# Attention ahead of two mixtures: two key blocks packed into one by an elementwise maximum, a third PSUM bank for products with v, gates and rank, and the rank behind the next scores

## The chip, the cores and the metric

One core of a Trainium2 chip runs the whole program. The metric is device time in microseconds (us), the median of several executions. The trace is one profiled execution of the kernel before; its times count from the first instruction. TensorE is called PE here, VectorE DVE, ScalarE ACT, GpSimd POOL, and SP is the engine that issues most DMAs.

## What is computed

Attention over 4 sequences of 576 positions with 8 heads of 64, causal within a window of 128 positions and with a slope per head, then a mixture with one chosen expert per row, then a mixture over four experts. The change touches the attention alone.

```python
def _attn_ref(q, k, v):
    B, H, S, D = q.shape          # 4, 8, 576, 64
    scores = (1.0 / np.sqrt(D)) * np.matmul(q, k.transpose(0, 1, 3, 2))
    rel = pos[:, None] - pos[None, :]
    bias = slopes[:, None, None] * (-np.abs(rel))[None, :, :]
    mask = (rel >= 0) & (rel < 128)
    scores = np.where(mask, scores + bias[None], -1000000000.0)
    attn = np.exp(scores - np.max(scores, axis=-1, keepdims=True))
    attn = attn / (np.sum(attn, axis=-1, keepdims=True) + 1e-09)
    return np.matmul(attn, v)
```

With a window of 128 and tiles of 128 positions, a row p of tile t sees the keys 0 to p of tile t and the keys p+1 to 127 of tile t-1: of each pair of columns c in the two key blocks exactly one is allowed, and the other holds a bias of about minus 1e12 times a slope.

## The kernel before

The 2304 rows make 18 tiles of 128 (`NTT`). The attention runs in 36 steps `s`, two to a tile (`t, hf = divmod(s, 2)`), each with four heads. Everything is recorded in program order, and each engine runs its own instructions in exactly that order, so a loop body further down is a queue for every engine at once. The loop of `attention()` (line 673 on) does in step s:

- `st_qk(s)` on PE: two bias matmuls and twelve score matmuls into `sc`, a PSUM tile of two banks (four heads times 256 keys, two buffers in `ps_s`). Queries and keys are split in a high and a low part (`qhi`, `qlo`, `khi`, `klo`).
- `st_max(s)` on DVE: the negated row maximum `nm` over 1024 elements of `sc`.
- `st_exp(s, jj)` on ACT: four exponentials of 256 keys, out of `sc` into `pr` in SBUF.
- `st_pv_t(s-1, jj)`: eight transposes of 128x128 on PE into `ps_t` (two buffers), and two copies of 512 elements to SBUF on ACT (`ptr`).
- `st_pv(s-2)` on PE: sixteen matmuls into `xo`, sum over keys of the probabilities times v (64 columns), a column of ones (the sum of probabilities) and eight columns of v times the gate's weights.
- `st_row(s-2)` on DVE: `den`, its reciprocal, the divided row `xrow` and the gate's part `lgh`.
- `st_vw(t)` in odd steps: eight small matmuls on PE and a copy on DVE.
- `split_k(t+1)` in even steps and `split_q(t+2)` in odd ones: high part and low part, both on DVE.
- in six steps (`SPLITS`) a weight of the first mixture is split: `whi` on ACT (line 134), in the next step `wlo` on DVE (line 138).

The first two steps of a sequence that begins at a tile's border (tiles 0 and 9, called open here) see one key block and have half of it all.

Beside this runs the routing (`st_route`, advanced one short instruction at a time by `route_op`): groups of one to three tiles get their expert by argmax and their place among the expert's rows by the rank matmuls `rkp` (line 573 on); DVE turns it into `row_i`, POOL scatters the rows to `xs` in memory by indirect DMA (line 606). Behind the scatter of the sixth group, tiles 14 and 15, three loads `early` bring the first expert's rows back (line 614); `first_rows` and `add_rows` put the first chunk of the mixture together from them and from the last two tiles, and with it the first mixture begins (matmuls `g`, line 766). `late_consts` builds constants and the bias tables of the sequences' borders on POOL, five pieces to a step.

PSUM has eight banks: four for `sc`, two for `ps_t`, two for `ps_m` (`xo`, `vw`, `rkp`).

## Time and profile before

| | |
|---|---|
| median of 3 runs | 1174.86 us (1173.76 to 1175.06) |
| the profiled execution's own time | 1174.67 us |
| its span, first to last instruction | 1172.6 us |
| PE busy | 1154.6 us, 98% |
| DVE busy | 778.6 us, 66% |
| ACT busy | 513.6 us, 44% |
| POOL busy | 92.6 us, 8% |
| mean granted PE clock | 0.997 of full speed |

The attention takes the first 182 us, the two mixtures the rest. The busy shares are means over both. Matmuls are pipelined, so a matmul's duration is longer than the distance from one start to the next; the distances are what adds up. A row of the trace's timeline gives start, duration of the merged instructions, engine, line, operation, out<-in, count, and in brackets the idle time of the engine ahead of it and what ended it.

### The profile page before, as it was taken

To read this page: it belongs to the slowest core of one execution; us is meant where nothing else is said; L and a number is where in the kernel's file an instruction comes from. 1 tells how busy PE (TensorE), PEld (TensorE's weight loads), DVE (VectorE), ACT (ScalarE), POOL (GpSimd) and SP (SyncE) were. 2 spreads that over 40 slices of the span, in tenths; PEclk is the share of its full clock that TensorE was granted. 3 is DMA by queue.
4 is the path that set the end of the run, shared out by engine and by line. 5 is a ranking of instruction groups with operands and counts; after the bars stand their busy time and mean duration, and the time that the engine had idled before them with its cause. 6 is when DMAs were issued, how large, how long until landed. Compare 5 with 4: busy or idle time off the path is not lost.

```text
span 1172.6 us, 17889 instructions
## 1 busy us (share of the span) xinstructions
PE 1154.6 (98%) x6914; PEld 1058.1 (90%) x6914; DVE 778.6 (66%) x1428; ACT 513.6 (44%) x928; POOL 92.6 (8%) x126
## 2 busy tenths in 40 slices
PE   8999999999999999999999999999999999999997
PEld 6888889999999999999998899999999899999996
DVE  6778865654665476666667876666667866666663
ACT  4565653554555453333334433344444433333331
POOL 8300010002310000000000200000000100000001
PEclk9999999999999999999999999999999999999999
DMA  9856434555575312222222322222112322222201
GB/s 306 279 157 204 136 100 154 169 175 168 160 226 162 94 55 72 73 72 73 72 72 60 103 73 72 73 72 72 59 68 72 108 72 72 72 72 73 72 18 54
DMA packets 62224, 126.58 MB, mean 108 GB/s; under 512 B 26272, under 2 KB 26272, under 8 KB 62112
## 3 DMA queue, kind: packets, MB, share of 16 engines
q1 hardware_dynamic: 58368, 114.96, 31.1%
q0 software_dynamic: 3456, 9.51, 2.1%
q8 instruction: 81, 1.33, 0.5%
q10 hardware_dynamic: 288, 0.52, 0.1%
q14 instruction: 31, 0.25, 0.1%
HBM read 109.18 MB, written 15.80 MB: 107 GB/s over the span
## 4 chain that ended last, share of the span: by engine, by line
issue 70%; PE 25%; POOL 2%; DVE 2%; DMA 1%; SPq 0%; POOLq 0%; ACT 0%
PE g L766 6%; PE y L871 6%; PE xo L463 5%; PE sc L420 2%; PE pt L448 2%; POOL out_dram L1296 2%; PE sc L412 1%; PE vw L523 1%; DMA rq<-in_q_dram 1%; PE xps L838 1%; DVE xrow L493 0%; DVE nm L429 0%; DVE qlo L253 0%; SPq L238 0%; DVE den L489 0%
## 5 line engine op out<-in xcount | busy, mean ns | idle before, releaser
L138 DVE TENSOR_TENSOR wlo<-raw,whi 128x1024 fp32r<-128x1024 f32 x160 | 193.4, 1221 | 129.6 <-ACT whi L134 129.6
L1275 PE MATMUL l<-whi,hhi 128*128 128x512 f32 x576 | 224.3, 389 | 1.6 <-DVE acc L1292 1.6
L1275 PE MATMUL l<-whi,hlo 128*128 128x512 f32 x576 | 224.6, 390 | 0.0
L1275 PE MATMUL l<-wlo,hhi 128*128 128x512 f32 x576 | 224.5, 390 | 0.0
L134 ACT CAST whi<-raw 128x1024 fp32r<-128x1024 f32 x160 | 165.7, 1055 | 131.9 <-DVE raw L160 106.1
L1188 ACT COPY x<-X 128x384 f32<-128x384 f32 x126 | 60.4, 480 | 269.2 <-PE X L1167 269.2
L1292 DVE SCALAR_TENSOR_TENSOR acc<-l,ct,acc 128x512 f32<-128x512 f32 x126 | 94.2, 747 | 81.7 <-PE l L1275 81.7
L1275 PEld LDWEIGHTS l<-whi,hhi 128*128 128x128 f32 x576 | 108.2, 188 | 24.4 <-DVE acc L1292 2.5
L1275 PEld LDWEIGHTS l<-whi,hlo 128*128 128x128 f32 x576 | 108.1, 188 | 22.5
L1275 PEld LDWEIGHTS l<-wlo,hhi 128*128 128x128 f32 x576 | 108.1, 188 | 21.9
L1193 DVE TENSOR_TENSOR x<-Z,x 128x384 f32<-128x384 f32 x84 | 44.7, 553 | 67.5 <-ACT x L1188 67.5
L1296 POOL DMA_INDIRECT out_dram<-acc,ctok x18 | 22.2, 1235 | 816.3 <-DVE acc L1292 488.2
L437 ACT ACTIVATE pr<-sc,nm 128x256 f32<-128x256 f32 (+1 forms) x144 | 58.9, 464 | 52.9 <-DVE nm L429 25.8
L1199 ACT ACTIVATE hhi<-x 128x384 fp32r<-128x384 f32 x126 | 58.1, 520 | 30.9 <-DVE x L1193 30.9
L871 PE MATMUL y<-hhi,whi 128*128 128x256 f32 (+2 forms) x224 | 69.6, 311 | 0.5 <-issue 0.5
L463 PE MATMUL xo<-vr,ptr 128*128 128x73 f32 x544 | 69.2, 279 | 0.2 <-ACT ptr L450 0.2
L871 PE MATMUL y<-hlo,whi 128*128 128x256 f32 (+2 forms) x224 | 69.0, 308 | 0.0
L871 PE MATMUL y<-hhi,wlo 128*128 128x256 f32 (+2 forms) x224 | 68.8, 307 | 0.0
L463 PEld LDWEIGHTS xo<-vr,ptr 128*128 128x128 f32 x544 | 63.7, 192 | 5.2 <-ACT ptr L450 0.5
L1205 DVE SCALAR_TENSOR_TENSOR hlo<-x,hhi 128x384 fp32r<-128x384 f32 x126 | 62.8, 552 | 2.7
L755 DVE SCALAR_TENSOR_TENSOR hlo<-g,hhi 128x384 fp32r<-128x384 f32 x64 | 35.1, 554 | 27.8 <-ACT hhi L754 26.3
L754 ACT ACTIVATE hhi<-g 128x384 fp32r<-128x384 f32 x64 | 31.2, 492 | 50.0 <-PE g L766 41.0
(348 smaller groups left out, 2555.2 us busy)
## 6 DMA issues: line engine op xcount, KB each, us to landing
raw<-in_w_b_dram SPq DMA_DIRECT2D x96, 512.0 KB, 3.6
raw<-in_w_a_dram SPq DMA_DIRECT2D x64, 512.0 KB, 3.8
xs<-zrow SPq DMA_DIRECT2D x8, 768.0 KB, 7.6
row<-xs SPq DMA_DIRECT2D x7, 768.0 KB, 5.1
rk<-in_k_dram SPq DMA_DIRECT2D x18, 256.0 KB, 4.5
vr<-in_v_dram SPq DMA_DIRECT2D x18, 256.0 KB, 4.2
rv<-in_vt_dram SPq DMA_DIRECT2D x18, 256.0 KB, 3.3
rq<-in_q_dram SPq DMA_DIRECT2D x16, 256.0 KB, 4.7
```

The source lines that it names most:

```text
L134: nc.scalar.copy(out=hi, in_=src)
L138: nc.vector.tensor_tensor(out=lo, in0=src, in1=hi.bitcast(F32), op=ALU.subtract)
L437: nc.scalar.activation(out=pr[:, r, jj, 0:w], in_=sc[s][:, r, jj, 0:w], func=AF.Exp, bias=nm[:, r, jj:jj + 1], scale=1.0,)
L463: nc.tensor.matmul(xo[:, 2 * jj + r, :], pt[:, r, c, :], vr[:, keys[c] % NSLOT, h, :], start=(c == 0), stop=(c == nk - 1),)
L766: nc.tensor.matmul(ps[:, 0:w], wl[:, c0:c0 + P], xl[dt // 2][:, dt % 2, 0:w], start=(dt == 0 and n == 0), stop=(dt == NDT - 1 and n == 2),)
L871: nc.tensor.matmul(acc[:, 0:w], wl[:, c0:c0 + P], hl[:, 0:w], start=(f == 0 and x == 0), stop=(f == NFT - 1 and x == 2),)
L1188: nc.scalar.copy(out=to, in_=xb[i])
L1199: nc.scalar.activation(out=hi, in_=c, func=AF.Relu)
L1205: nc.vector.scalar_tensor_tensor(out=lo, in0=c, scalar=0.0, in1=hi.bitcast(F32), op0=ALU.max, op1=ALU.subtract)
L1275: nc.tensor.matmul(acc, hl[:, ts], wl[:, c0:c0 + DM], start=(m == 0 and x == 0), stop=(m == 3 and x == 2),)
L1292: nc.vector.scalar_tensor_tensor(out=accs[g], in0=acc, scalar=pe, in1=accs[g], op0=ALU.mult, op1=ALU.add)
L1296: nc.gpsimd.indirect_dma_start(out=outv[g], out_offset=bass.IndirectOffsetOnAxis(ap=ctok[:, g, :], axis=0), in_=accs.pop(g), in_offset=Non ...
```

## The change

In `st_max` ACT copies the first key block's scores out of PSUM into `pr` (now 512 elements to a step, three buffers), DVE takes the elementwise maximum of the second block and that copy into `pr`, and the row maximum of the 512 results; in open steps the row maximum is taken from PSUM directly. `st_exp` makes four exponentials of 128 elements in place. `st_turn(s-2)` makes four transposes instead of eight into one bank (`ps_t` has one buffer now), ACT copies them out once, and POOL writes two masked copies by `affine_select`, one with the columns of each key block. `st_pv(s-3)` makes the same sixteen matmuls on these, one step later than before, so the loop has one step more (`ns + 3`). `ps_m` has three banks. From tile 2 on, the high parts of q and k are made on ACT. The late bias tables are made on ACT, three pieces to a step (`late_biases`), and no longer on POOL. The rank matmuls of the first six groups are held until the next step, behind its scores and transposes (`held`).

```diff
-            ps_t = actx.enter_context(tc.tile_pool(name="ps_t", bufs=2, space=PSUM))
-            ps_m = actx.enter_context(tc.tile_pool(name="ps_m", bufs=2, space=PSUM))
+            ps_t = actx.enter_context(tc.tile_pool(name="ps_t", bufs=1, space=PSUM))
+            ps_m = actx.enter_context(tc.tile_pool(name="ps_m", bufs=3, space=PSUM))
...
-                nc.vector.tensor_copy(out=khi[:, :, c, :], in_=rk)
+                if t < 2:
+                    nc.vector.tensor_copy(out=khi[:, :, c, :], in_=rk)
+                else:
+                    nc.scalar.copy(out=khi[:, :, c, :], in_=rk)
...
-                nc.vector.tensor_scalar(out=hi, in0=rq, scalar1=0.125, scalar2=None, op0=ALU.mult)
+                if t < 2:
+                    nc.vector.tensor_scalar(out=hi, in0=rq, scalar1=0.125, scalar2=None, op0=ALU.mult)
+                else:
+                    nc.scalar.activation(out=hi, in_=rq, func=AF.Copy, scale=0.125)
...
+            def late_biases():
+                for h in range(H):
+                    for o, w in ((0, 2 * P), (2 * P, P)):
+                        build_bias(1, h, o, w)
+                        yield
+                for h in range(H):
+                    build_bias(2, h, 0, 2 * P)
+                    yield
+                for h in range(H):
+                    build_bias(0, h, 2 * P, P)
+                    yield
...
             def st_max(s):
-                w = len(geom(s // 2)[0]) * P
+                scores = sc.pop(s)
+                pr = spool.tile([P, 2, 2, P], F32, tag="pr", name=f"pr{s}", bufs=3)
+                if len(geom(s // 2)[0]) == 2:
+                    nc.scalar.copy(out=pr, in_=scores[:, :, :, 0:P])
+                    nc.vector.tensor_tensor(out=pr, in0=scores[:, :, :, P:], in1=pr, op=ALU.max)
+                    scores = pr
+                else:
+                    scores = scores[:, :, :, 0:P]
                 nm = small.tile([P, 2, 2], F32, tag="nm", name=f"nm{s}")
-                nc.vector.tensor_reduce(out=nm, in_=sc[s][:, :, :, 0:w], axis=AX.X, op=ALU.max, negate=True)
...
+                nc.vector.tensor_reduce(out=nm, in_=scores, axis=AX.X, op=ALU.max, negate=True)
+                prob[s] = pr, nm, scores
...
+            def st_turn(s):
+                keys = geom(s // 2)[0]
+                pr, _, _ = prob.pop(s)
+                ps = ps_t.tile([P, 4, P], F32, tag="t", name=f"pt{s}")
+                for i in range(4):
+                    nc.tensor.transpose(ps[:, i, :], pr[:, i % 2, i // 2, :], ident)
+                both = spool.tile([P, 4, P], F32, tag="pt", name=f"pt{s}")
+                nc.scalar.copy(out=both, in_=ps)
...
+                for d in range(2):
+                    part = spool.tile([P, 4, P], F32, tag=f"pt{d}", name=f"pt{s}_{d}")
+                    nc.gpsimd.affine_select(
+                        out=part, in_=both, pattern=[[0, 4], [1 - 2 * d, P]], base=-d, channel_multiplier=2 * d - 1,
+                        compare_op=ALU.is_ge, fill=0.0,
                     )
+                    probt[s][s // 2 - d] = part
...
+                if t0 < LATE:
+                    yield "rank"
                 pr = ps_m.tile([P, m + 1, E1], F32, tag="m", name=f"rkp{g}")
...
-            for s in range(ns + 2):
+            for s in range(ns + 3):
...
                     st_max(s)
-                    st_exp(s, 0)
-                route_op()
-                if s == ns + 1:
+                if 2 <= s < ns + 2:
+                    st_turn(s - 2)
+                if s < ns:
+                    st_exp(s)
+                route_op(rank=True)
+                if s == ns + 2:
                     while back:
-                        route_op()
+                        route_op(rank=True)
                     first_rows(0)
...
+                if s >= 3:
+                    st_pv(s - 3)
+                    st_row(s - 3)
```

What this makes of the queues is seen at three places. First ACT in steps 14 and 15 (`pr14` is the probabilities of step 14, `pt13` the transposed ones of step 13, `khi` and `qhi` the high parts). Before:

```order
L437 ACTIVATE pr14_1157<-sc14_1140,nm14_1155 128x256 x2
L450 COPY ptr13_0_1183<-pt13_0_1178 128x512
L437 ACTIVATE pr14_1157<-sc14_1140,nm14_1155 128x256 x2
L450 COPY ptr13_1_1192<-pt13_1_1187 128x512
L437 ACTIVATE pr15_1235<-sc15_1218,nm15_1233 128x256 x2
L450 COPY ptr14_0_1269<-pt14_0_1264 128x512
L437 ACTIVATE pr15_1235<-sc15_1218,nm15_1233 128x256 x2
L450 COPY ptr14_1_1278<-pt14_1_1273 128x512
```

After:

```order
L436 COPY pr14_1103<-sc14_1088 128x512
L461 COPY pt12_1113<-pt12_1108 128x512
L449 ACTIVATE pr14_1103<-pr14_1103,nm14_1106 128x128 x4
L246 CAST khi_122<-rk8_890 128x4x128
L436 COPY pr15_1170<-sc15_1155 128x512
L461 COPY pt13_1180<-pt13_1175 128x512
L449 ACTIVATE pr15_1170<-pr15_1170,nm15_1173 128x128 x4
L258 ACTIVATE qhi9_1214<-rq9_1021 128x512
```

ACT's queue now begins a step with a copy of the scores and ends it with a high part, and the copy of the next step's scores stands behind both.

Second, DVE in the second half of step 14, up to the row maximum of step 15 (`den`, `xrow`, `lgh`, `lg` are `st_row` and the gate, `oh`, `rk`, `row_i`, `base`, `key` and `mx` are routing). Before:

```order
L571 TENSOR_TENSOR oh_all_75<-key1_1113,km1_1114 128x24
L243 CAST khi_122<-rk8_936 128x4x128
L244 TENSOR_TENSOR klo_123<-rk8_936,khi_122 128x4x128
L588 TENSOR_TENSOR rk1_1115<-rkp1_1200,oh_all_75 128x24
L591 TENSOR_REDUCE row_i_76<-rk1_1115 128x3
L592 COPY base_73<-rkp1_1200 128x8
L429 TENSOR_REDUCE nm15_1233<-sc15_1218 128x4
```

After, the whole of step 14 up to the maximum of step 15:

```order
L437 TENSOR_TENSOR pr14_1103<-sc14_1088,pr14_1103 128x512
L442 TENSOR_REDUCE nm14_1106<-pr14_1103 128x4
L505 TENSOR_SCALAR den11_1132<-xo11_1123 128x4
L506 RECIPROCAL den11_1132<-den11_1132 128x4
L510 TENSOR_TENSOR xrow5_1077<-xo11_1123,den11_1132 128x256
L527 TENSOR_TENSOR lgh5_1082<-xo11_1123,den11_1132 128x32
L552 TENSOR_REDUCE lg1_872<-lgh5_1082 128x8
L573 TENSOR_REDUCE mx1_1141<-lg1_872 128x3
L247 TENSOR_TENSOR klo_123<-rk8_890,khi_122 128x4x128
L582 TENSOR_TENSOR key1_1142<-lg1_872,mx1_1141 128x24
L584 TENSOR_TENSOR key1_1142<-key1_1142,kc_338 128x24
L437 TENSOR_TENSOR pr15_1170<-sc15_1155,pr15_1170 128x512
```

The maximum of step 15 (`pr15`) stands behind `klo`, which reads the `khi` that ACT makes behind the exponentials of step 14; before the change DVE made both splits itself, one right behind the other, and the row maximum read `sc` directly.

Third, PE around the last scores of the attention, `sc35`: where the rank of the sixth group (`rkp5`) stands. Before:

```order
L448 MATMUL pt33_0_2527<-ident_71,pr33_2441 128x128 x4
L448 MATMUL pt33_1_2536<-ident_71,pr33_2441 128x128 x4
L574 MATMUL rkp5_2543<-base_73,top_706 128x24
L578 LDWEIGHTS tri_625
L578 MATMUL rkp5_2543<-oh_all_75,tri_625 128x24
L580 LDWEIGHTS ones_704
L580 MATMUL rkp5_2543<-oh_all_75,ones_704 128x16
L580 LDWEIGHTS ones_704
L580 MATMUL rkp5_2543<-oh_all_75,ones_704 128x8
L412 LDWEIGHTS identb_174
L412 MATMUL sc35_2563<-bias0_177,identb_174 128x512
```

After:

```order
L459 MATMUL pt34_2533<-ident_71,pr34_2431 128x128 x4
L593 MATMUL rkp5_2544<-base_73,top_280 128x24
L597 LDWEIGHTS tri_273
L597 MATMUL rkp5_2544<-oh_all_75,tri_273 128x24
L599 LDWEIGHTS ones_278
L599 MATMUL rkp5_2544<-oh_all_75,ones_278 128x16
L599 LDWEIGHTS ones_278
L599 MATMUL rkp5_2544<-oh_all_75,ones_278 128x8
L480 MATMUL xo33_2550<-vr_124,pt33_0_2499 128x73
L480 MATMUL xo33_2550<-vr_124,pt33_1_2501 128x73
```

The rank stood ahead of `sc35` and stands behind it, behind the transposes of step 34 and behind the product of step 32; the product of step 33 follows. And POOL at the same place, before:

```order
L606 DMA xs_69<-xrow13_2123,row_i_76 18433x512
L606 DMA xs_69<-xrow14_2255,row_i_76 18433x512
L606 DMA xs_69<-xrow15_2395,row_i_76 18433x512
L606 DMA xs_69<-xrow16_2517,row_i_76 18433x512
L606 DMA xs_69<-xrow17_2638,row_i_76 18433x512
L824 MEMSET zb_2807 128x384
```

After:

```order
L468 AFFINE_SELECT pt33_0_2499<-pt33_2497 128x512
L468 AFFINE_SELECT pt33_1_2501<-pt33_2497 128x512
L468 AFFINE_SELECT pt34_0_2540<-pt34_2538 128x512
L468 AFFINE_SELECT pt34_1_2542<-pt34_2538 128x512
L625 DMA xs_69<-xrow14_2267,row_i_76 18433x512
L625 DMA xs_69<-xrow15_2406,row_i_76 18433x512
L468 AFFINE_SELECT pt35_0_2592<-pt35_2590 128x512
L468 AFFINE_SELECT pt35_1_2594<-pt35_2590 128x512
L625 DMA xs_69<-xrow16_2523,row_i_76 18433x512
L625 DMA xs_69<-xrow17_2606,row_i_76 18433x512
L847 MEMSET zb_2763 128x384
```

The scatter of tiles 14 and 15 (`xrow14`, `xrow15`) now stands between the masked copies of step 34 and those of step 35.

## Rows read from the trace of the kernel before

**Rows 1.** Busy time by stretch: length, PE, PEld, DVE, ACT, POOL, clock, DMA.

```profile
20.00:165.00 145.00, 143.76 (x1333) 126.08 (x1334) 115.79 (x327) 87.27 (x202) 30.40 (x51) 1.00 0.58 185
```

**Rows 2.** Timeline of PE in one step, and the start of step 35.

```profile
105.55 2.01 PE L463 MATMUL xo<-vr,ptr 128*128 128x73 f32 x16
107.40 1.04 PE L448 MATMUL pt<-ident,pr 128*128 128x128 f32 x8
108.27 0.59 PE L412 MATMUL sc<-bias,identb 128*128 128x512 bf16 x2
...
164.83 0.59 PE L412 MATMUL sc<-bias,identb 128*128 128x512 bf16 x2
```

**Rows 3.** Groups of ACT by form, 0 to 185 us: busy, mean ns, idle before.

```profile
L450 ACT COPY ptr<-pt 128x512 f32<-128x512 f32 x64 | 37.8, 592 | 16.1 <-PE pt L448 14.6 <-PE vw L523 1.1
L134 ACT CAST whi<-raw 128x1024 fp32r<-128x1024 f32 x6 | 6.5, 1076 | 0.0
L437 ACT ACTIVATE pr<-sc,nm 128x128 f32<-128x128 f32 x16 | 4.9, 367 | 4.3 <-DVE nm L429 4.3
L300 ACT ACTIVATE bias<-rel 128x256 bf16<-128x256 f32 x8 | 2.6, 401 | 0.0
```

**Rows 4.** Groups of DVE by form, 0 to 185 us.

```profile
L244 DVE TENSOR_TENSOR klo<-rk,khi 128x512 fp32r<-128x512 f32 x18 | 12.5, 696 | 0.6
L138 DVE TENSOR_TENSOR wlo<-raw,whi 128x1024 fp32r<-128x1024 f32 x6 | 7.3, 1218 | 0.0
L429 DVE TENSOR_REDUCE nm<-sc 128x4 f32<-128x512 f32 x4 | 2.8, 690 | 1.2 <-PE sc L420 1.2
```

**Rows 5.** Timeline of ACT and DVE: a run of exponentials, one handover.

```profile
8.11 1.76 ACT L437 ACTIVATE pr<-sc,nm 128x128 f32<-128x128 f32 x6 [2.51 <-DVE nm L429]
...
25.47 0.84 ACT L437 ACTIVATE pr<-sc,nm 128x256 f32<-128x256 f32 x2 [1.38 <-DVE nm L429]
...
24.15 1.23 DVE L429 TENSOR_REDUCE nm<-sc 128x4 f32<-128x1024 f32 x1 [0.59 <-ACT ptr L450]
```

**Rows 6.** POOL's selects by form, one POOL copy and one `klo` in the timeline.

```profile
L276 POOL TENSOR_SCALAR_AFFINE_SELECT rel<-rel 128x256 f32<-128x256 f32 x2 | 0.8, 398 | 0.1
...
11.54 0.89 POOL L326 COPY rel<-rel 128x256 f32<-128x256 f32 x1
...
18.07 0.77 DVE L244 TENSOR_TENSOR klo<-rk,khi 128x512 fp32r<-128x512 f32 x1
```

**Rows 7.** DVE in step 2; two stretches as in rows 1.

```profile
15.53 1.22 DVE L429 TENSOR_REDUCE nm<-sc 128x4 f32<-128x1024 f32 x1 [0.83 <-PE sc L420]
...
11.60:14.00 2.40, 0.61 (x3) 0.10 (x1) 2.34 (x4) 0.10 (x1) 2.26 (x3) 1.00 1.11 362
...
17.30:19.60 2.30, 2.30 (x14) 1.40 (x14) 1.50 (x4) 1.66 (x6) 2.08 (x4) 0.50 1.08 411
```

**Rows 8.** End of the attention: DVE, POOL, SP, landing of `early`, PE.

```profile
163.68 0.16 DVE L488 TENSOR_SCALAR den<-xo 128x4 f32<-128x4 f32 x1 [0.63 <-PE xo L463]
...
165.00 0.18 DVE L588 TENSOR_TENSOR rk<-rkp,oh_all 128x16 f32<-128x16 f32 x1 [0.31 <-PE rkp L580]
165.22 0.17 DVE L591 TENSOR_REDUCE row_i<-rk 128x2 int32<-128x16 f32 x1
...
166.37 1.23 DVE L429 TENSOR_REDUCE nm<-sc 128x4 f32<-128x1024 f32 x1 [0.91 <-PE sc L420]
...
165.66 0.97 POOL L606 DMA_INDIRECT xs<-xrow,row_i  x1 [15.93 <-DVE base L592]
...
169.77 1.28 SPq L614 DMA_DIRECT2D early<-xs  x3
...
DMA to landing us min/median/max: 2.6/2.7/2.8
...
173.58 0.60 PE L625 MATMUL xps<-ident,early 128*128 128x128 f32 x4
...
182.29 0.41 PE L766 MATMUL g<-x0('s', 0)_0_2751,whi 128*128 128x384 f32 x1 [1.55 <-ACT x0('s', 0)_1_2752 L185]
```

More of the change, by code (lines that the diff above doesn't have):

```diff
@@ L318, in attention @@
             rc = {}
+            def late_biases():
[9 more added lines that the diff above has]
+                    yield
             def late_consts():
-                for h in range(H):
-                    build_bias(0, h, 2 * P, P, nc.gpsimd)
-                    yield
                 for x in (1, 2):
@@ L442, in st_pv_t @@
-            def st_pv_t(s, jj):
-                nk = len(geom(s // 2)[0])
-                pr, _ = prob[s]
-                ps = ps_t.tile([P, 2, 2, P], F32, tag="t", name=f"pt{s}_{jj}")
-                for r in range(2):
-                    for c in range(nk):
-                        nc.tensor.transpose(ps[:, r, c, :], pr[:, r, jj, c * P:(c + 1) * P], ident)
-                pt = spool.tile([P, 2, 2, P], F32, tag="pt", name=f"ptr{s}_{jj}", bufs=4)
-                nc.scalar.copy(out=pt[:, :, 0:nk], in_=ps[:, :, 0:nk])
-                probt[s, jj] = pt
+                scores = sc.pop(s)
@@ new lines, in st_max, with st_exp @@
+                prob[s] = pr, nm, scores
+            def st_exp(s):
+                pr, nm, scores = prob[s]
+                for jj in range(2):
+                    for r in range(2):
+                        nc.scalar.activation(
+                            out=pr[:, r, jj, :], in_=scores[:, r, jj, :], func=AF.Exp,
+                            bias=nm[:, r, jj:jj + 1], scale=1.0,
+                        )
+            def st_turn(s):
[6 more added lines that the diff above has]
+                nc.scalar.copy(out=both, in_=ps)
+                if len(keys) == 1:
+                    probt[s] = {s // 2: both}
+                    return
+                probt[s] = {}
+                for d in range(2):
[3 more added lines that the diff above has]
+                        compare_op=ALU.is_ge, fill=0.0,
+                    )
+                    probt[s][s // 2 - d] = part
@@ L664, in offsets, with route_op @@
                 nc.vector.tensor_copy(out=off_i, in_=off[0:1])
-            back, late, consts = [], [], late_consts()
-            def route_op():
+            back, late, consts, extra = [], [], late_consts(), late_biases()
+            held = []
+            def route_op(rank=False):
                 todo = gates if gates and (not back or gates[0][0] < back[0][0]) else back
-                if todo and next(todo[0][1], True):
+                if not todo or (held and not rank):
+                    return
+                held.clear()
+                got = next(todo[0][1], "end")
+                if got == "end":
                     todo.pop(0)
-            for s in range(ns + 2):
+                elif got == "rank":
+                    held.append(todo)
+            for s in range(ns + 3):
                 t, hf = divmod(s, 2)
@@ L721, in attention @@
                         domain_probs()
-                    for _ in range(5):
-                        if next(consts, True):
-                            pass
+                    for todo in (consts, consts, extra, extra, extra):
+                        next(todo, None)
                 route_op()
```

68 lines of the change are left out of this document (19 added, 49 removed).

## Prediction

> **What bounds the kernel now.** I read three views. First the busy time by stretch: between 20 and 165 us PE is busy 143.76 of 145.00 us at full clock, DVE 115.79, ACT 87.27 and POOL 30.40 [rows 1]. The attention is bound by PE, and DVE has a fifth of its time left. Second the timeline of PE: in a step the product with v takes 1.85 us from its start to that of the transposes, the eight transposes 0.87 us to that of the next scores, and from the scores of step 23 to those of step 35 twelve steps take 56.56 us, 4.71 us each [rows 2]. Third the groups by form on ACT and DVE, for the durations that the new instructions are priced with [rows 3, 4]. What lies behind 182.29 us, where the first matmul of the first mixture starts [rows 8], is the same code before and after; a difference reaches the end through that moment alone, apart from the clock.
>
> **What comes off PE.** Four of eight transposes in 32 steps: 32 x 0.87 / 2 = 13.9 us. If PE stays the bound, a step is 4.71 - 0.44 = 4.27 us. That is what the change has to offer, and only if ACT and DVE can deliver a step in 4.27 us.
>
> **What comes onto ACT and DVE: a loop.** Before, a step's row maximum needed nothing but the scores. After, there is a circle through both engines, since both run in order: DVE's maximum of step s+1 stands behind the low part (`klo` or `qlo`) of step s; that waits for the high part, which ACT makes behind the exponentials of step s; these wait for DVE's row maximum of step s. One turn of the circle, by rows:
> - Maximum of two operands, 512 elements. No row shows it from PSUM. The nearest is the two-input `klo` at 0.696 [rows 4]; ends 0.65 and 0.77, I take 0.69. The next instruction starts 0.05 later (165.00 + 0.18 to the next at 165.22 is 0.04 [rows 8]).
> - Row maximum over 512: 0.690 [rows 4].
> - Handover DVE to ACT: 24.15 + 1.23 = 25.38, start at 25.47, so 0.09 [rows 5].
> - Four exponentials of 128: six take 1.76 with 0.367 for the last, so 0.28 from start to start [rows 3, 5]; 4 x 0.28 = 1.12 until ACT is free for the next.
> - High part on ACT, 512 elements, no row: between 0.401 (256) and 1.076 (1024) on a straight line 0.63 [rows 3].
> - Handover 0.09, then the low part 0.696 [rows 4].
> The sum is 0.69 + 0.05 + 0.69 + 0.09 + 1.12 + 0.63 + 0.09 + 0.70 = 4.06; I take **4.0**, with ends 3.8 and 4.15 from the ends of the maximum, of the exponentials and of the high part. ACT's way round, where the copy of the scores (0.592, as the copies of 512 out of PSUM [rows 3]) stands in the place of the low part, is about 0.1 shorter.
>
> That is under 4.27, but it is a bare turn. On it come, over steps 2 to 35:
> - The bias tables, now behind the high part on ACT: 25 to 27 pieces of steps 2 to 10, at 2.6 / 8 = 0.33 for 256 elements [rows 3] and some 0.22 for 128 (estimate from that row and the 0.28 above), 7 us; ACT has 0.1 to 0.2 of slack in each of nine turns, and 5 to 6 remain.
> - Six weight splits: `whi` 1.08 [rows 3] less that slack, and `wlo` 1.22 [rows 4] in the next step, in front of the maximum: 6 x (0.95 + 1.15) = 12.6, where PE hid all of it before.
> - About 21 short routing instructions on DVE that stand between low part and maximum, 0.16 each as in [rows 8]: 3.4.
> - Less: two open steps without copy and maximum (2 x 0.73) and the last two without splits (2 x 0.65): -2.8.
> Together about 18. The row maximum of step 2 should end at 17.6: its scores are complete at 15.53 as before [rows 7], then 0.09 + 0.59 + 0.05 + 0.69 + 0.05 + 0.69 = 2.1. Then that of step 35 ends at 17.6 + 33 x 4.0 + 18 = **167.6**. Before it ended at 166.37 + 1.23 = 167.60 [rows 8]. **The main stage gives back all of the 13.9 us**: PE's work is less, and PE waits in each step instead.
>
> **Edits that I cost at nothing on this way.** The copies on ACT out of `ps_t` (half as many) and the single buffer of `ps_t`: the copy stands right behind that of the scores, a step ahead of the next transposes. POOL's masked copies: the nearest rows are a select of 256 at 0.398 and a copy of 256 at 0.89 [rows 6], so 0.6 to 1.8 for one of 512; I take 0.62, two fit into a step of 4.5 even at 1.8, and one step of delay of the product covers them. If that cover went, PE would wait for POOL. The third bank of `ps_m` and the held rank of the first five groups take waits from PE that are now no longer the bound: between 0 and -1.
>
> POOL now works in each step, beside DVE. In the one place where the timeline shows a POOL copy shortly ahead of a `klo`, that takes 0.77 and not the mean 0.696 [rows 6]; I take no price for it, as one row is little. The Trainium skill, "GPSIMD Engine Reference" (section 8, Key points), says that POOL shares its SBUF interfaces with VectorE and that DVE instructions with two SBUF inputs contend; that speaks against this change, which puts selects beside `klo` and `qlo`. By that rule 33 low parts would be 0.08 longer, 2.6 us, and the time 1184.5.
>
> **The end of the attention.** Here the later rank counts. Before: the sixth group's `row_i` came at 165.39, ahead of the last row maximum; the scatter started 0.27 later at 165.66, the load `early` was issued at 169.77, 4.11 behind, and lands 2.7 later at 172.5; the first transposes on it started at 173.58, so it was just in time [rows 8]. After, the rank is behind the scores and row maximum of step 35 and DVE makes `oh` behind them: 167.6 + about 1.3 (`km`, `vr`, `den`, reciprocal, `xrow`, `lgh`, `oh`, of the widths in [rows 8]) = 168.9. PE then does the rank and the product of step 33, 2.0 [rows 2]: 170.9. DVE's `row_i` stands behind the `den` to `lg` of step 33: +1.4 (163.68 to 165.39 less the wait of 0.31) = 172.3. Then +0.27 + 4.11 = 176.7 for the load's issue and +2.7 = 179.4 for its landing. The first transposes wait until then, and the last product with v stands behind them on PE. From there as before 182.29 - 173.58 = 8.7: the first mixture starts at 188.1, **+5.8 us**. Ahead of 179.4 PE has only two products and four transposes, and idles some 4 to 6 us. In the one place of the trace with such a gap, 11.6 to 14.0 with PE busy 0.61 of 2.40, the granted clock fell behind it: 0.83 and then 0.50, which is 1.2 GHz, from 17.3 to 19.6 with PE busy throughout [rows 7]. At half rate this cost 2.3 / 2 = 1.15. I add **1.2**. The Trainium skill, "TensorE: Matmul & The Clock Gate" (section "Why this matters for your kernels"), warns of idle gaps between bursts of matmuls; the row agrees.
>
> **Sum.** 0.0 + 5.8 + 1.2 = +7.0 on the profiled execution's own 1174.67, so 1181.7; the median stands 0.2 above it (1174.86): **1182**.
>
> **Rivals.**
> 1. *PE keeps the pace*: ACT and DVE run the circle in 4.2 with all extras hidden. This needs the exponentials, high and low parts to overlap far more than rows 3 to 5 let them; against it stands that mean turn, 4.0 + 18 / 33 = 4.5. For it: ACT at 87.27 and DVE at 115.79 of 145 have room if only busy time counts [rows 1]. Then all 13.9 is kept and the longer end still costs 7.0: 1174.86 - 13.9 + 7.0 = 1168. Faster.
> 2. *The turn is 3.8*: its lower end, from the shorter end of each term. 33 x 0.2 = 6.6 less: 1175.4. No change. It is also what comes out if the early rows land sooner than I work out while the loop is as forecast (-5.8 - 1.2: 1175).
> 3. *The clock falls in the attention*: PE now idles in each step (4.5 - 4.27, in steps with a weight split over 1 us). At 1.2 GHz a step's 4.27 us of work takes 8.5, 4.0 more than the turn; four such steps give +16: 1198. For it the row at 17.3; against it that the gap ahead of it was longer than any I expect inside the loop.
>
> **How the numbers follow.** The forecast has 0.55, with own range 1176 to 1189 from a turn of 3.85 to 4.15; rival 1 0.17, rival 2 0.20, rival 3 0.08. Only differences over 0.2% (2.3 us) can be told from none. Faster: rival 1 and 0.05 of rival 2, 0.22. Same: 0.14 of rival 2 and 0.06 of the forecast, 0.20. Slower: the rest, 0.58. The range that leaves out rival 3, half of what lies beyond rival 1 and little of the forecast is 1167 to 1189.
>
> **What would show it.** Loop: ACT waits for `nm`, DVE's maximum and low part wait for ACT, PE waits in each step for `pr` or `sc`, its busy share from 20 to 150 falls to some 94%, and the step is 4.5 us. Rival 1: PE 99% busy and a step of 4.27. End: `row_i` of the sixth group some 5 us behind the last row maximum, the first transposes of `early` waiting for a DMA, PE idle for 4 us ahead of them and a clock under 1.00 behind. The select should show at 0.6. The forecast is wrong if the last row maximum ends before 162, if the high parts on ACT take under 0.5, or if `early` lands ahead of the last product with v.

## The result and the profile after

The changed kernel takes 1183.12 us, the median of 8 executions from 1180.15 to 1188.37. Against the kernel before, 1175.03 us beside it, the ratio is 1.0076 (95% interval 1.0054 to 1.0098): slower by about 8 us, forecast 1182. Where before all executions lay within 3 us, they now spread over 8. The profiled one is the longest of them, 1188.37 us with a span of 1185.7; it is 13.7 above the profiled execution of before, and the accounts below are of these two.

First the busy time by stretch of the changed kernel (length; busy time and number of instructions of PE, weight loads, DVE, ACT, POOL; granted clock; share and GB/s of the DMAs).

```profile
20.00:165.00 145.00, 138.03 (x1178) 116.99 (x1178) 106.77 (x311) 98.35 (x253) 52.32 (x71) 0.93 0.56 184
...
20.00:45.00 25.00, 21.71 (x189) 17.87 (x189) 15.12 (x40) 20.00 (x56) 4.93 (x9) 0.99 0.87 302
45.00:58.00 13.00, 13.00 (x67) 10.88 (x67) 8.44 (x23) 8.37 (x25) 2.44 (x4) 0.50 0.33 107
58.00:115.00 57.00, 55.35 (x515) 47.68 (x514) 45.21 (x136) 39.46 (x98) 22.82 (x29) 1.00 0.59 186
115.00:130.00 15.00, 13.43 (x94) 11.01 (x94) 9.89 (x29) 7.73 (x21) 6.30 (x8) 0.77 0.36 122
130.00:165.00 35.00, 34.54 (x324) 29.56 (x321) 28.10 (x85) 22.79 (x56) 15.83 (x21) 1.00 0.48 150
```

Before, the clock was 1.00 over the whole of 20 to 165 us and PE idled 1.24 us [rows 1]. Now PE idles 6.97 us there, and the clock is 0.93: from 45 to 58 us PE is busy throughout at 0.50, which is 1.2 GHz, and again for a part of 115 to 130. Lost clock, length times what is missing to 1.00, is 145 x 0.07 = 10.2 us, 6.5 of them from 45 to 58 alone. A second execution of the same code up to step 34, that of the run e3_end below, shows nearly the same sums: 6.64 us idle and a clock of 0.94.

What PE did ahead of these two stretches, in its timeline (start, duration, engine, line, operation, tiles, in brackets the idle time ahead and what ended it), and two late steps from scores to scores:

```profile
27.71 0.66 PE L459 MATMUL pt<-ident,pr 128*128 128x128 f32 x4 [1.60 <-ACT pt L461]
...
42.44 0.66 PE L459 MATMUL pt<-ident,pr 128*128 128x128 f32 x4 [0.98 <-ACT pt L461]
...
118.86 3.82 PE L480 MATMUL xo<-vr,pt 128*128 128x73 f32 x16 [1.43 <-POOL pt L468]
...
158.69 0.60 PE L418 MATMUL sc<-bias,identb 128*128 128x512 bf16 x2
...
163.25 0.59 PE L418 MATMUL sc<-bias,identb 128*128 128x512 bf16 x2
...
166.94 0.59 PE L418 MATMUL sc<-bias,identb 128*128 128x512 bf16 x2
```

PE waits for ACT in steps 5 and 8 (some expectations below call the first of them step 6) and for POOL's masked copy in step 24. Late steps are as short as PE alone would make them: 163.25 to 166.94 is 3.69, and 158.69 to 163.25 with the small products for v is 4.56. The same two kinds of step before the change:

```profile
104.12 0.59 PE L412 MATMUL sc<-bias,identb 128*128 128x512 bf16 x2
108.27 0.59 PE L412 MATMUL sc<-bias,identb 128*128 128x512 bf16 x2
...
113.31 0.59 PE L412 MATMUL sc<-bias,identb 128*128 128x512 bf16 x2
```

These take 4.15 and 5.04, so a step without waits and rank is 0.46 to 0.48 shorter now, 4.12 in the mean and not 4.60. (The 4.71 of the prediction is the mean of twelve steps, some of which hold rank matmuls too.) Yet the last scores start at 166.94, 2.1 later than before [rows 2].

One turn of the circle between DVE and ACT, steps 4 to 5, from the maximum of one step to that of the next:

```profile
27.21 0.69 DVE L437 TENSOR_TENSOR pr<-sc,pr 128x512 f32<-128x512 f32 x1 [0.48 <-ACT pr L436]
...
27.94 0.69 DVE L442 TENSOR_REDUCE nm<-pr 128x4 f32<-128x512 f32 x1
...
28.66 1.28 ACT L449 ACTIVATE pr<-pr,nm 128x128 f32<-128x128 f32 x4 [1.00 <-DVE nm L442]
...
29.84 0.60 ACT L246 CAST khi<-rk 128x512 fp32r<-128x512 f32 x1
...
30.35 0.92 ACT L304 ACTIVATE bias<-rel 128x256 bf16<-128x256 f32 x3
30.48 0.69 DVE L247 TENSOR_TENSOR klo<-rk,khi 128x512 fp32r<-128x512 f32 x1 [0.71 <-ACT khi L246]
...
31.18 0.56 ACT L436 COPY pr<-sc 128x512 f32<-128x512 f32 x1
...
31.77 0.69 DVE L437 TENSOR_TENSOR pr<-sc,pr 128x512 f32<-128x512 f32 x1 [0.60 <-ACT pr L436]
```

The turn takes 31.77 - 27.21 = 4.56 with three pieces of the bias tables in it; by way of `klo`, without them, it would end at 31.17, 3.96 behind its start. ACT itself waits 1.00 us for `nm` in the middle of this turn.

And the end (DVE, POOL, SP, landing of the early rows, PE), which answers to [rows 8]:

```profile
170.46 0.69 DVE L442 TENSOR_REDUCE nm<-pr 128x4 f32<-128x512 f32 x1
...
176.04 0.16 DVE L610 TENSOR_REDUCE row_i<-rk 128x2 int32<-128x16 f32 x1
...
176.48 0.99 POOL L625 DMA_INDIRECT xs<-xrow,row_i  x1 [2.08 <-DVE mxl L573]
...
180.53 1.28 SPq L633 DMA_DIRECT2D early<-xs  x3
...
183.13 1.12 PE L644 MATMUL xps<-ident,early 128*128 128x128 f32 x4 [4.11 <-DMA early<-xs]
...
194.86 0.41 PE L789 MATMUL g<-x0('s', 0)_0_2707,whi 128*128 128x384 f32 x1 [1.39 <-ACT x0('s', 0)_1_2708 L185]
```

The row maximum of step 35 ends at 171.15 (before 167.60), the first mixture starts at 194.86 (before 182.29). So 3.6 of the 12.6 us were lost up to the last row maximum, and 9.0 behind it. From the first matmul of the mixture to the end of the span it is 990.8 us, before 990.3.

### The profile page after: what moved, and what is told of

Its sections match the earlier page's. It is cut to its first block, busy times and chain, and to the rows that moved or that the text cites. A ratio compares the mean times of both kernels' runs of the same rounds, so it can differ in the third digit from the quotient of the medians.

```text
span 1185.7 us, 17746 instructions
## 1 busy us (share of the span) xinstructions
PE 1157.8 (98%) x6785; PEld 1057.4 (89%) x6786; DVE 773.0 (65%) x1428; ACT 527.5 (44%) x988; POOL 112.3 (9%) x158
## 4 chain that ended last, share of the span: by engine, by line
issue 71%; PE 20%; POOL 3%; DVE 3%; ACT 2%; DMA 1%; POOLq 0%; ACTq 0%; SPq 0%; DVEq 0%
PE g L789 6%; PE y L894 6%; PE xo L480 3%; PE sc L426 2%; POOL out_dram L1319 2%; ACT pr L449 1%; PE pt L459 1%; PE sc L418 1%; DVE nm L442 1%; PE vw L540 1%; POOL pt L468 1%; DVE pr L437 1%; PE xps L861 1%; POOL xs L625 0%; ACT pr L436 0%
## 5 line engine op out<-in xcount | busy, mean ns | idle before, releaser
L1298 PEld LDWEIGHTS l<-whi,hhi 128*128 128x128 f32 x576 | 108.2, 188 | 24.4 <-DVE acc L1315 2.5
L480 PE MATMUL xo<-vr,pt 128*128 128x73 f32 x544 | 74.4, 292 | 3.6 <-POOL pt L468 2.0
L480 PEld LDWEIGHTS xo<-vr,pt 128*128 128x128 f32 x544 | 69.6, 206 | 5.9 <-POOL pt L468 5.9
L449 ACT ACTIVATE pr<-pr,nm 128x128 f32<-128x128 f32 x128 | 40.9, 390 | 39.1 <-DVE nm L442 39.1
```

The costliest lines, as they stand in the source:

```text
L449: nc.scalar.activation(out=pr[:, r, jj, :], in_=scores[:, r, jj, :], func=AF.Exp, bias=nm[:, r, jj:jj + 1], scale=1.0,)
L480: nc.tensor.matmul(xo[:, i, :], pt[c][:, i, :], vr[:, c % NSLOT, 4 * hf + i, :], start=(n == 0), stop=(n == len(pt) - 1),)
L1298: nc.tensor.matmul(acc, hl[:, ts], wl[:, c0:c0 + DM], start=(m == 0 and x == 0), stop=(m == 3 and x == 2),)
```

## The experiments

Each run below changes the changed kernel, or a version built on it, and its name stands in brackets; the intervals of the ratios are 95%. Three theories are set against each other. Theory A: the turn of the circle is not the bound in most steps; single waits of PE come from work that stands at the wrong place on ACT, DVE and POOL, and behind them the clock falls, which costs more than the waits. Theory B, the prediction's: the circle with its extras paces PE in each step. Theory C: the clock falls for a reason of its own.

**The bias tables in ACT's hole.** (run e1_bias) ACT waits 1.00 us ahead of the exponentials, its hole; the pieces are put there.

```diff
                     st_turn(s - 2)
+                if 1 <= s < ns:
+                    for _ in range(3):
+                        next(extra, None)
...
-                    for todo in (consts, consts, extra, extra, extra):
+                    for todo in (consts, consts):
```

> The changed kernel, with the three pieces of the bias tables per step moved on ACT from behind the high part to between the copy of the transposed probabilities and the exponentials, where ACT waited 1.00 us for the row maximum in every step. Theory A (gap and clock): the pieces made PE wait 1.6 us in step 6 and about 1 us in step 8, and the fall of the clock to 0.50 between 45 and 58 us follows from these gaps. Then the steps up to the first weight split go at PE's own 3.7 and 4.6 us, that stretch at 0.50 is gone or short, and the time falls by 7 to 9 us, to 1174 to 1176. Theory B (the loop of the prediction as the bound everywhere): only the 5 to 6 us of the pieces themselves come back, 1177 to 1178, PE waits in each step as before, and the clock is as before.

Measured: 1178.53 us (1174.85 to 1182.89), ratio to before 1.0033 (1.0017 to 1.0048). By stretch:

```profile
20.00:45.00 25.00, 25.00 (x233) 21.43 (x231) 17.90 (x45) 22.29 (x61) 6.85 (x11) 1.00 0.91 313
45.00:65.00 20.00, 18.79 (x120) 16.01 (x120) 12.24 (x43) 13.50 (x37) 6.77 (x9) 0.67 0.49 149
```

From 20 to 45 us PE no longer waits at all (before this edit 3.3 us), and the steps 6 to 10 go at 3.67 and 4.56. But the next wait of PE, 1.21 us at 50.4 us for the first group's one-hot (`oh_all`, a row's choice of expert as zeros and a one, which DVE makes and the rank matmuls read), now has the fall behind it. 4.6 us came back, fewer than A expected; B's figure of 5 to 6 is nearer. What speaks for A is where they came from: PE has no waits left in the steps with pieces, where B had it wait in each.

**The weight splits in the holes too.** (run e2_hole) `whi` goes to the same place on ACT a step later, `wlo` ahead of the low part on DVE.

```diff
+                if s - 1 in SPLITS:
+                    w_split(late)
                 if s < ns:
                     st_exp(s)
...
+                if late:
+                    late.pop(0)()
                 if s < ns:
                     if hf == 0:
                         if 2 <= t + 1 < NTT:
```

> As e1_bias, and the weight splits too: the high part of the weight stands in the same place on ACT (one step later), and its low part ahead of the low part of q or k on DVE, where DVE waited 0.9 us. Theory A: with both moved, PE keeps its pace but for the steps with scatters on POOL; no stretch at clock 0.50 before 110 us, the last scores start at 153 to 158 and not at 166.9, and the time is 1168 to 1172. Theory B: the bare turn of 4.0 us stays the bound together with the short instructions on DVE; the last scores start at 160 or later, 1175 or more.

Measured: 1184.27 us (1181.44 to 1186.25). The last scores start at 163.57, and the time is B's by its number, but not by its cause: the steps go at 3.67 to 4.56 up to 80 us, and the waits for ACT are gone. What took their place, as a wait of PE (total, times, longest), on POOL and by stretch:

```profile
PE xo L480 <- POOL pt L468: 3.9, 4, 1.6
```

```profile
78.25 1.45 POOL L625 DMA_INDIRECT xs<-xrow,row_i  x1 [1.72 <-DVE base L611]
80.00 0.97 POOL L625 DMA_INDIRECT xs<-xrow,row_i  x1 [0.31 <-issue]
81.28 0.98 POOL L625 DMA_INDIRECT xs<-xrow,row_i  x1 [0.30 <-issue]
82.26 3.80 POOL L468 TENSOR_SCALAR_AFFINE_SELECT pt<-pt 128x512 f32<-128x512 f32 x4
```

```profile
80.00:100.00 20.00, 18.29 (x114) 16.04 (x114) 10.28 (x27) 7.76 (x22) 6.97 (x8) 0.66 0.49 150
```

Three scatters of a group stand in a row on POOL, the masked copies of two steps queue behind them, PE waits for these (3.9 us in four places), and the clock is 0.66 over 20 us. Two of the places are here, two near 117 us.

**The end alone.** (run e3_end) The routing of the sixth group is run up to its one-hot in step 34, its rank and row numbers in step 35, and the first transposes of the early rows stand behind the last product with v.

```diff
                     st_row(s - 3)
+                if s == 2 * LATE + 2:
+                    while back and not held:
+                        back_op()
+                if s == ns + 2:
+                    first_rows(0)
...
-                route_op(rank=True)
+                if s == 2 * LATE + 3:
+                    held.clear()
+                    back_op()
+                    back_op()
+                else:
+                    route_op(rank=True)
```

> The changed kernel with its end alone mended: the routing of the sixth group is run on DVE up to its one-hot in one go in step 34, its rank stands in step 35 behind the transposes of step 33 and its row numbers behind the last row maximum, and the first transposes on the early rows stand behind the last product with v. Theory A (the later rank costs the end): the load of the early rows is issued about 5 us after the last row maximum and not 9.4, the wait of 4.1 us on PE is gone, the clock stays up behind it, and the time falls by 6 to 9 us, to 1174 to 1177. Rival (the landing is late anyway, because the scatters stand behind POOL's selects): it falls by under 2.5 us.

Measured: a median of 1182.06 us, 1.1 under the changed kernel and so the rival's by its number. There are two kinds of execution: five of ten from 1173.39 to 1179.41, five from 1184.70 to 1186.78. The wait for the early rows is gone from PE, which only A had. In the profiled one, of the longer kind, a shorter wait took its part:

```profile
168.25 0.17 PE L597 MATMUL rkp<-oh_all,tri 128*128 128x24 bf16 x1 [0.98 <-DVE oh_all L588]
```

```profile
165.00:192.00 27.00, 24.41 (x141) 23.16 (x140) 15.04 (x64) 7.64 (x21) 9.01 (x12) 0.68 0.19 68
```

PE is busy 24.4 of 27 us there, at a mean clock of 0.68. The shorter executions show a gain of up to 10 us; the longer ones have the lower clock, 0.975 to 0.983 in the mean over the whole execution where the shorter have 0.982 to 0.994. No trace of a shorter one was kept, so that the clock takes the gain back is read from these means and the trace above.

**All three, and the scatters one to a step.** (run e4_all) A `yield "rank"` stands between the scatters of the first four groups, which holds the next until the next step.

> e2_hole and e3_end together, and the scatters of the first four groups one to a step, so that POOL's selects wait for one scatter of 1.3 us and not for three. Theory A: the gains add, the clock is 1.00 from 20 us on to the first mixture, the last scores start at 152 to 156, and the time is 1158 to 1164, faster than the kernel before. Theory B: the loop holds the attention, 1168 or more.

Measured: 1169.46 us (1165.75 to 1173.85), ratio 0.9958 (0.9944 to 0.9973): faster than before, though by its number B's (1168 or more). The last scores start at 150.01, sooner than A had them, so the loop does not hold the attention. The clock is 1.00 from 20 to 163 us and falls once more, behind a wait of 1.38 for the seventh group's one-hot; that wait and the clock behind it, 8 x 0.43 = 3.4, are most of the 5.5 us that are missing to A's 1164. PE's waits for POOL are 0.3 us here, in e2_hole 3.9; the spaced scatters were not run by themselves.

```profile
163.00:171.00 8.00, 7.88 (x41) 7.88 (x41) 3.91 (x20) 0.41 (x1) 0.99 (x1) 0.57 0.36 132
```

**Work in the gaps.** (runs e5_fill and e9_fill2) Nothing is moved; PE gets matmuls whose results nobody reads, where it waited.

```diff
+                if s in (6, 8, 10):
+                    busy(ps_m, "m", 6)
                 if 2 <= s < ns + 2:
                     st_turn(s - 2)
...
+                if s in (22, 23, 24):
+                    busy(ps_m, "m", 6)
                 if s >= 3:
                     st_pv(s - 3)
```

> The changed kernel with nothing moved, but with six additional matmuls of 512 columns on PE, into a bank of the third kind that is free, ahead of the transposes in steps 6, 8 and 10 and ahead of the product with v in steps 22, 23 and 24: work whose results nobody reads, where the trace of the changed kernel shows PE waiting ahead of the two falls of the clock inside the attention. It adds 36 matmuls of 0.21 us, 7.7 us of work at full clock, a part of it inside waits. Theory A (the gaps let the clock fall, and the fall costs more than the gaps): the stretches at 0.50 between 45 and 58 and between 117 and 126 us shrink or go, which gives back up to 10 us; the time falls by 2 to 6 us although PE does more, with the fall at the end, near 180 us, unchanged. Theory C (the clock falls for another reason, not for the gaps): the two stretches stay and the time rises by 4 to 8 us.

> The changed kernel with 20 additional matmuls on PE in place of the 36 of e5_fill: five each ahead of the transposes in steps 6 and 8 and ahead of the product with v in steps 23 and 24. In e5_fill the clock stayed at 1.00 from 20 to 165 us and the last scores came 6.8 us earlier than in the changed kernel, but ahead of the first mixture PE stood for 4.5 us that the profile puts down to PE's own queue at the loads of the counts. If that wait comes with the place of the code that the longer PE program moved, it is gone here or changed; then theory A (gaps let the clock fall) has the time at 1177 to 1181, below the changed kernel's 1183 although PE does 4.3 us more. If the wait is there again, 1182 to 1186. Theory C (the clock falls for another reason): falls at 45 and 117 us as in the changed kernel, 1186 to 1188.

The first, with 36 matmuls, by stretch and at the start of the mixture:

```profile
20.00:45.00 25.00, 24.72 (x216) 20.06 (x216) 16.11 (x42) 20.01 (x56) 4.95 (x9) 1.00 0.85 300
45.00:58.00 13.00, 12.65 (x118) 10.55 (x114) 10.41 (x33) 9.65 (x29) 4.20 (x7) 1.00 0.48 143
...
115.00:130.00 15.00, 15.00 (x136) 13.01 (x135) 11.67 (x32) 10.49 (x25) 4.28 (x8) 1.00 0.41 124
```

```profile
191.13 0.66 PE L793 MATMUL g<-x0('s', 0)_0_2749,whi 128*128 128x384 f32 x1 [4.46 <-PEq L922]
```

Both falls inside the attention are gone, and the last scores start at 160.18, 6.8 us sooner than in the trace of the changed kernel although PE did more. That trace is of its longest execution, and the wait of step 5 stands ahead of the first added matmuls; it was 0.28 us here before any of them ran. The trace of e3_end is the better comparison: its code is that of the changed kernel up to step 34, its wait in step 5 is 0.36, and in step 8 it has

```profile
40.78 0.66 PE L459 MATMUL pt<-ident,pr 128*128 128x128 f32 x4 [0.99 <-ACT pt L461]
```

and behind that a clock of 0.50 near 45 us, another fall from 115 to 128 us, and its last scores at 165.05. Against it the added matmuls gain 4.9 us, and the two falls are gone. This supports A and speaks against C. Yet the time is 1185.78 (1185.35 to 1186.53): behind the unchanged fall at the end stands a new wait of 4.46 us on PE's own queue at the loads of the counts. With 20 matmuls that wait is not there, the last scores start at 159.53, and the time is 1180.54 (1179.35 to 1186.15), inside A's 1177 to 1181. The two falls are gone here too; a short one, 0.52 to 0.63 from 54 to 58 us, stands behind a wait of 1.31 for the one-hot. By their times alone neither run can be told from the changed kernel: the ratios to before, 1.0076 to 1.0110 and 1.0035 to 1.0076, overlap with its 1.0054 to 1.0098. Where the 4.46 comes from was not settled.

**Banks as before the change**, two and two. (run e6_banks)

> The changed kernel with the banks as before: two for the transposed probabilities, two for the products with v, gates and rank. The prediction priced the one buffer for the transposes at nothing; the trace of the changed kernel has PE waiting there three times, 2.8 us in all, up to 1.6, for ACT's copy of the step before. If these waits come from the single buffer, they go, and with them perhaps the fall of the clock near 45 us: 3 to 9 us less, 1174 to 1180. If they come from ACT being late anyway, or the two other banks make PE wait for DVE in turn, the time stays within 3 us of the changed kernel's 1183.

Measured: 1180.42 us (1178.72 to 1181.66), within 3 us of the changed kernel. The waits for ACT's copy are gone; PE waits for DVE instead, and behind the wait below the clock is 0.50 to 0.53 from 29 to 36 us:

```profile
28.53 3.11 PE L480 MATMUL xo<-vr,pt 128*128 128x73 f32 x16 [1.28 <-DVE lgh L527]
```

So the single buffer for transposes had a part in waits of 2.8 us, which the prediction put at nothing. It is not enough for them by itself: in e1_bias, with one buffer, they are gone as well, because ACT's copies come sooner. With two banks for the products PE waits for DVE in their place.

**High parts on DVE as before.** (run e7_highdve)

> The changed kernel with the high parts of q and k on DVE again, as before the change: the circle through ACT is opened, and DVE has 0.43 us more in each step. By the loop of the prediction a step's turn goes from 4.0 to about 3.4 plus the bias pieces, and DVE's own sum to about 4.1; the early gaps of PE (steps 6 and 8) shrink, and the time falls by 3 to 8 us, to 1175 to 1180. If DVE is the bound then (weight splits and routing on top of 4.1), PE waits for the row maximum in the steps 11 to 33 and the time rises by up to 10 us.

Measured: 1177.19 us (1172.75 to 1182.21), ratio to before 1.0017 (1.0001 to 1.0034). That is 5.9 us under the changed kernel, as expected. With the circle opened, steps 6 to 10 go at PE's pace; the falls at the splits and scatters (105 to 125 us at 0.74) and at the end stay.

**The version that beats both.** (run e8_best) e4_all, with the high parts also ahead of the exponentials, routing ahead of the gates, the sixth group's rank behind the small products for v, and the last product with v ahead of the seventh group's rank.

```diff
                     st_turn(s - 2)
+                if s < ns:
+                    if hf == 0 and 2 <= t + 1 < NTT:
+                        high_k(t + 1)
+                    elif hf == 1 and t + 2 < NTT:
+                        high_q(t + 2)
...
-                todo = gates if gates and (not back or gates[0][0] < back[0][0]) else back
+                todo = gates if gates and not back else back
```

> e4_all with the high parts of q and k also moved ahead of the exponentials on ACT, the routing ahead of the gates, the rank of the sixth group behind the small products for v and the last product with v ahead of the rank of the seventh. In e4_all PE waited 3.6 us for the rank's one-hot, 1.4 of them near 162 us, and the clock fell to 0.50 behind that. Theory A: that fall goes and with it 3 to 5 us; the last scores start at 148 to 150, and the time is 1161 to 1166 with less spread than the 1166 to 1174 of e4_all. Rival (other gaps take their place): 1168 to 1171 as e4_all.

Measured: 1159.22 us (1157.50 to 1159.72), ratio 0.986 (0.9843 to 0.9877).

```profile
20.00:165.00 145.00, 143.94 (x1336) 125.40 (x1334) 118.34 (x376) 107.77 (x273) 59.54 (x83) 1.00 0.61 197
```

```profile
PE g L829 <- ACT x0('s', 0)_1_2708 L185: 1.4, 1, 1.4
```

The clock is 1.00 from 20 us to the mixture and beyond, PE's longest wait is the one it had before the change as well [rows 8], the last scores start at 147.35 and the mixture at 166.38. So once nothing gives it back, the change brings the last scores 17.5 us sooner than before; 32 steps that are 0.47 shorter make 15.0 of it, and the rest was not traced to its place.

**The price of one gap.** (run e10_gap) e8_best with `whi` made five more times in step 12.

> The price of one gap by itself: e8_best with the high part of the second weight made six times over on ACT in step 12 (5 x 1.05 = 5.3 us more, the same values), so that the exponentials of step 12 come late and PE runs out of work once, near 58 us. PE can cover 1 to 3 us of it and waits 2 to 4. Theory A: behind that gap the clock shows a stretch at 0.50 of 8 to 13 us, which costs 4 to 6.5 beside the gap: the time is 1159 + 2 to 4 + 4 to 6.5 = 1165 to 1170. Theory C: the gap alone, 1161 to 1163, and no stretch under 1.00.

Measured: 1166.91 us (1165.71 to 1168.56), 7.7 more. The wait on PE (total, times, longest), the stretch from 63 to 79 us, and below it the same stretch of e8_best:

```profile
PE sc L440 <- DVE klo L255: 2.4, 1, 2.4
```

```profile
63.00:79.00 16.00, 13.08 (x86) 10.58 (x85) 10.29 (x30) 11.96 (x28) 3.65 (x6) 0.79 0.44 148
```

```profile
63.00:79.00 16.00, 16.00 (x156) 14.19 (x155) 13.30 (x45) 12.72 (x31) 6.69 (x11) 1.00 0.53 167
```

PE idles 16 - 13.08 = 2.9 us, and the clock of 0.79 loses another 16 x 0.21 = 3.4. This gap costs about as much again behind it, 6.3 in all, as A has it and C does not. The other 1.4 are no part of it: in the profiled executions the scores of step 4 start at 23.11 here and at 21.72 in e8_best, well ahead of the edit.

**The third bank and the held rank, without other falls.** (runs e11_banks and e12_unheld) e8_best with the banks of before, and e8_best with the rank of the first five groups not held:

> e8_best with the banks as before the change, two for transposes and two for the products with v, gates and rank: the price of the third bank where the clock no longer covers it. e6_banks moved the changed kernel by about -3 us, with the falls of the clock at other places. If the third bank is worth what it seems to be for (products of one step while DVE still reads the last), two banks cost 1 to 2 us in waits of PE for DVE, the steps with rank and with the small products above all, 1160 to 1162. If the second buffer for transposes is worth more: 1157 to 1159. A fall of the clock through the new waits would add 4 or more.

> e8_best with the rank of the first five groups not held until the next step: it stands behind its one-hot at once, as before the change. DVE makes that one-hot at the end of a step; PE would wait for it ahead of the next scores, 0.3 to 1.6 us in each of five places. Expected: 1160 to 1163, more if one of the waits lets the clock fall; if PE's lead covers it, 1159 as e8_best.

Measured: 1168.30 us (1166.41 to 1168.85) and 1169.70 (1167.54 to 1170.31), 9.1 and 10.5 more than e8_best. With the banks of before PE has no new wait from 20 to 145 us; two waits at the end are enough, the first ahead of the product of step 32 (below it a row of DVE):

```profile
152.93 2.38 PE L492 MATMUL xo<-vr,pt 128*128 128x73 f32 x16 [0.85 <-POOL pt L480]
...
152.62 0.21 DVE L553 COPY vr<-vw 128x64 f32<-128x64 f32 x1
```

The profile names POOL, but POOL's copies end at 152.96, behind the start of the product. With two banks the product takes the one that `vw` of step 35 had (`vw`, rank, product, in this order), and DVE's copy out of it ends at 152.83, 0.10 ahead. With three banks, in e8_best, the same product starts at 150.39, ahead of that copy at 151.07. So this wait is for the bank.

```profile
153.00:172.00 19.00, 18.25 (x97) 18.19 (x97) 8.31 (x40) 3.70 (x11) 5.76 (x7) 0.55 0.25 84
```

The clock is 0.55 for 19 us, with the second wait, of 0.75, inside. Not held, the rank makes PE wait in five places, with a fall behind the longest:

```profile
PE rkp L609 <- DVE oh_all L600: 5.7, 5, 2.0
```

```profile
95.00:105.00 10.00, 8.03 (x55) 6.27 (x56) 6.56 (x26) 5.35 (x13) 2.83 (x4) 0.66 0.81 267
```

So in this version the third bank and the held rank are worth some 9 and 10 us. Of the first the two waits are 1.6, and most of the rest is clock (in its profiled execution 1.4 were lost ahead of step 4, as in e10_gap). Of the second 5.7 are the waits and about 5 the clock: 10 x 0.34 = 3.4 here, and 5 x 0.34 = 1.7 near 170 us, behind a wait of 1.09 for the early rows. Both expectations were too low, since they priced the waits and gave the fall only as an addition.

## Why the prediction came out right, and where its steps did not

**The number was right, one half of its reason was not.** 1183.12 against 1182, inside the range and on the forecast side. The profiled execution, the longest, is 6.7 above the 1181.7 that was worked out for it; 3.6 of that were lost up to the last row maximum and 2.0 between it and the mixture.

**Right: what comes off PE.** 0.44 us a step was forecast; 0.46 and 0.48 were measured in the two kinds of step.

**Right: the length of the turn.** 4.0 was forecast, 3.96 measured; the terms lie at 0.69 for the maximum (0.69), 1.18 up to the high part (1.12), 0.60 for the high part (0.63), 0.69 for the low part (0.70).

**Wrong: "the main stage gives back all of the 13.9 us" through the circle.** The step that failed is the sum, 33 x 4.0 + 18 (its extras add up to 18.2 to 19.2): it lets the circle set every step and puts the clock at nothing within the attention. The bare turn of 4.0 is below PE's own 4.1, as the prediction itself noted for 4.27; in such steps PE sets the pace, and the extras only count by what they exceed PE's slack. Where the bias pieces stood the circle did set the pace, 4.56 a turn; moving them gave 4.6 us (e1_bias), opening the circle 5.9 (e7_highdve). PE waited 5.7 us more than before between 20 and 165 us, not 14. The rest of what was given back is the clock, 10.2 us, the third rival with 0.08. The two came to nearly the sum that the circle alone was to cost. The row maximum of step 2 ends at 18.93 + 0.69 = 19.62, where 17.6 was forecast, and that of step 35 at 171.15 and not 167.6: 151.5 us between them, forecast 150.0. That this agrees is luck, two errors that offset each other. Rivals 1 and 3 were worked out as if they excluded each other; here most steps went at PE's pace, and the falls of the clock took back what that gained.

**Wrong: the single buffer for transposes and POOL's masked copies at nothing.** The price of one copy was right, 0.62 forecast and 0.635 as the median:

```profile
L468 POOL TENSOR_SCALAR_AFFINE_SELECT pt<-pt x64: 624/635/1683, 27.7 to 179.3; 128x512 f32<-128x512 f32 x64
```

What the step left out is what else stands in POOL's queue: a group's three scatters hold it for some 4 us, from 113.93 to 118.14, and the cover of one step is then gone (1.43 at 118.86, and the second fall). It named the loss of cover and didn't look for it. The single buffer had its part in the waits for ACT, 2.8 us, as e6_banks shows.

**POOL beside DVE.** The Trainium skill, "GPSIMD Engine Reference" (section 8, Key points), has DVE instructions with two SBUF inputs contend with POOL. The 2.6 us worked out from it did not come: over the changed kernel the low parts of q have

```profile
L259 DVE SCALAR_TENSOR_TENSOR qlo<-rq,qhi x16: 681/693/1068, 15.7 to 156.7; 128x512 fp32r<-128x512 f32 x16
```

a median of 0.693, near the 0.696 of [rows 4]: from 20 to 162 us 27 of the 31 low parts stand beside no masked copy. Of the four that do, the trace agrees for two, and with a larger price than 0.08: behind a masked copy that had begun first they take 1.07 (at 92.43) and 0.99 (at 148.06). The two that began ahead of the copy take 0.68 and 0.69.

**Right: the end.** `row_i` 4.7 us behind the last row maximum was forecast, 5.05 measured; scatter to load 4.11 and 4.05; landing 11.8 behind the row maximum and 11.98; PE's wait 4 to 6 and 4.11. Mis-sized was the clock behind it: 1.2 forecast, but from the first transposes on the early rows to the mixture it took 11.7 us and before 8.7, so 3.0; the clock is 0.66 in these 11.7.

## What to carry to other kernels

A circle through two engines that is a little shorter than the bounding engine's step is no bound: add up what exceeds the slack, place by place, and not the whole of it. Put side work where an engine waits anyway, and read the queue of every engine that a new step uses for what else stands in it. On a stage that PE bounds, price a new wait together with the clock behind it.

## What had not been expected of the hardware

In these traces waits of 0.85 to 2.4 us were followed by a mean clock of 0.50 to 0.79 over stretches of 8 to 27 us: one wait of 2.4 us and one of 0.45 behind it cost some 6 us in e10_gap, and with waits of 0.85 and 0.75 e11_banks took 9.1 longer. It isn't the same each time: in e12_unheld the wait of 2.0 us had a fall behind it, and the four others for the rank, 3.7 in all, had none, the wait of 1.4 us ahead of the mixture has none in e8_best, and equal executions of e3_end differ by 13 us. The spread of a kernel's executions is no sure sign: it is 8 us in the changed kernel and 2.2 in e8_best, which has no such waits within the attention, but 1.2 in e5_fill and 2.4 in e11_banks, which have them. Nor does the mean clock order the changed kernel's executions: 1180.15 us has 0.984 and 1188.37 has 0.985, so what makes them differ by 8 us is open.
